# Weights in chunks of 768 columns, the second layer's by rows, half of them converted during attention

## Chip, cores and metric

One Trainium2 chip, one of its NeuronCores. The metric is the device time of one execution in microseconds. Engines are named TensorE (PE; PEld is its weight load), VectorE (DVE), ScalarE (ACT), GpSimd (POOL) and SyncE (SP, whose queue issues the transfers here).

## What is computed

Attention with a tanh cap over 2 batches, 12 heads, 448 positions and 64 channels; its output, 896 tokens by 768, goes through two feed-forward networks. All inputs are float32.

```python
scores = cap * np.tanh(scale * (q @ k.T) / cap)
attn = softmax(scores)                            # sum + 1e-9
x = (attn @ v) as [896, 768]

h = x @ w_in                                      # 768 -> 1024
solu = h * softmax(h)
ln = (solu - mean) / np.sqrt(var + 1e-6) * g_ln
x = ln @ w_out                                    # 1024 -> 768, the second layer

gate = sigmoid(x @ w_gate)                        # 768 -> 1536
out = (gate * (x @ w_val)) @ w_out2               # 1536 -> 768
```

## The kernel before

Every product of the networks is computed as three products of float32r operands (hi times hi, hi times lo, lo times hi), so weights and activations are split into a rounded upper part and the rest. The weights reach the kernel as 64-bit words. A chunk of 512 columns (`CH`, line 37) is loaded by SP into one of three raw buffers (`chunk_load`, line 308) and converted in six steps (`chunk_steps`, line 317): a mask of the upper word (line 349 on VectorE, or line 347 on ScalarE with `act=True`), a clamp (352), a shift (353), two merging steps on VectorE (354, 355), of which the second also rounds the upper part on ScalarE (`upper`, 336), and the subtraction of the rounded part on VectorE (`lower`, 339). For the second layer's weights `upper` first multiplies by the norm's weight `g_ln` on VectorE (334), since a chunk holds four blocks of 128 rows side by side for one block of 128 outputs. There are 12 chunks of w_in, 12 of w_mid (the second layer's weights), 36 of w_gv (gate and value) and 18 of w_fin.

`chunk_stream` (361) puts the steps of several chunks, interleaved, into a queue `todo`, and `fill(k)` issues the next k of them. A load goes out at the last step of the chunk three before it (`AHEAD`).

Attention (from line 520) runs in slots, two per pair of heads, each with half of the keys of that pair: scores on TensorE (`s_mm`), tanh and exp on ScalarE, the weighted sums on TensorE (`s_pv`); at each odd slot the sums are copied out (`s_out`) and turned into reciprocals through small transfers (`n_recip`), and GpSimd multiplies (`n_mult`). Slots 0 to 15 issue 5 conversion steps each (`FILL`), which are those of w_in. In slot 16 the stream of w_mid starts and five slots issue one step each. From slot 16 on the first layer of token tiles 0 and 1 runs beside attention (`beside`).

The loop over token tiles 2 to 6 (line 587) does the first layer's 36 products for a tile, then the maximum (`ln_max`), exp (`ln_exp`, line 420), the product h times exp (423), statistics, the norm (`ln_norm`, 441), and one tile later the transposes (`ln_trans`, 449) and the split into ln_hi and ln_lo (`ln_evac`). The buffer of exp and norm is a single one, so a tile's exp waits for the transposes of the tile before. Each round issues four conversion steps: after 18 of the products, after `ln_exp`, after `x_split` of the tile two ahead (on GpSimd, 392), and after `ln_norm`; tile 6 has its own order.

The second layer (`l2`, line 637) computes one block of 128 outputs for one of two token groups (384 and 512 columns), 24 products each. It needs the two chunks of its output block and calls `fill` until they are there, and 4 more steps after its products. Up to line 666 the order of the instructions on TensorE, ScalarE, VectorE and GpSimd is the order of the code; SP's order and all that follows (`load_slabs`, the gated layer, the last layer) is ordered by the compiler's planner.

Of the kernel before, what the change touches and what calls it, by code (L numbers as in the profile page):

```python
# [10 lines left out]
F32 = mybir.dt.float32  # L11
# [25 lines left out]
CH = 4 * P  # L37
# [6 lines left out]
AHEAD = 3  # L44
W2_BUFS = 9
# [8 lines left out]
FILL = 5  # L54
S_W2 = 16
FILL_T = 1
FILL_2 = 4
# [24 lines left out]
def fused_kernel(ctx: ExitStack, tc: tile.TileContext, qk, v, cap, w_in, w_mid, g_ln, w_gv, w_fin, outT):  # L82
# [5 lines left out]
    sh.wraw = ctx.enter_context(tc.tile_pool(name="wraw", bufs=3, side="right"))  # L88
    sh.cvt = ctx.enter_context(tc.tile_pool(name="cvt", bufs=3, side="right"))
# [53 lines left out]
def network(ctx: ExitStack, tc: tile.TileContext, sh, general, w_in, w_mid, w_gv, w_fin, outT):  # L143
# [10 lines left out]
    lns = ExitStack()  # L154
    lnt1 = lns.enter_context(tc.tile_pool(name="lnt1" + sfx, bufs=1, side="right"))
# [3 lines left out]
    lin = lns.enter_context(tc.tile_pool(name="lin" + sfx, bufs=1, side="right"))  # L159
    lin2 = lns.enter_context(tc.tile_pool(name="lin2" + sfx, bufs=2, side="right"))  # L160
    wi, x0 = ExitStack(), ExitStack()
    wip = wi.enter_context(tc.tile_pool(name="wi" + sfx, bufs=1, side="left"))
    x0p = x0.enter_context(tc.tile_pool(name="x0" + sfx, bufs=1, side="left"))
    wi_hi = wip.tile([P, K1, F1], F32R, name="wi_hi")
    wi_lo = wip.tile([P, K1, F1], F32R, name="wi_lo")
    x_sb = [x0p.tile([P, NP, S], F32, name="x0"), lin.tile([P, NP, S], F32, name="x1")]
# [150 lines left out]
    def chunk_steps(get, dst, scale=None, act=False):  # L317
# [43 lines left out]
    def chunk_stream(chunks):  # L361
# [16 lines left out]
        todo.extend(step for _, _, step in sorted(order, key=lambda x: x[:2]))  # L378
# [16 lines left out]
    def l1_mms(t):  # L395
# [3 lines left out]
        def mm(half, kk, m):  # L399
# [4 lines left out]
            c = slice(half * 512, half * 512 + 512)  # L404
            nc.tensor.matmul(hts[t][:, half], l[:, kk], r[:, kk, c], start=(kk == 0 and m == 0), stop=(kk == K1 - 1 and m == 2))  # L405
# [60 lines left out]
    def wi_dst(kk, half):  # L466
        c = slice(half * CH, half * CH + CH)
        return lambda: (wi_hi[:, kk, c], wi_lo[:, kk, c], None)
# [5 lines left out]
    chunk_stream([(w_in[:, kk, h * CH:(h + 1) * CH], wi_dst(kk, h), None) for h in range(2) for kk in range(K1)])  # L474
# [31 lines left out]
    def w2_dst(m, c):  # L506
        def dst():
            hl = w2p.tile([P, 2, 4, P], F32R, tag="w", name="w_hl")
            return hl[:, 0].rearrange("p a b -> p (a b)"), hl[:, 1].rearrange("p a b -> p (a b)"), lambda: w2[m].append(hl)
        return dst  # L510

    w2 = [[] for _ in range(K3)]
# [74 lines left out]
    for t in range(L1_BESIDE, 7):  # L587
        if t == 3:
            x0.close()
        if t == 2:  # L590
# [3 lines left out]
            w2p = lns.enter_context(tc.tile_pool(name="w2p" + sfx, bufs=W2_BUFS, side="right", reuse_waits="tile"))  # L594
# [12 lines left out]
        if t == 6:  # L607
# [4 lines left out]
            fill(3 * k)  # L612
# [12 lines left out]
        fill(k)  # L625
# [4 lines left out]


    def prod(out, w, kw, xh, xl, kx, first, last):
        wh, wl = w[kw // 4][:, 0, kw % 4], w[kw // 4][:, 1, kw % 4]
        for m, (l, r) in enumerate(((wh, xh), (wh, xl), (wl, xh))):
            nc.tensor.matmul(out, l, r[kx], start=(first and m == 0), stop=(last and m == 2))  # L635

    def l2(m, g):
        while len(w2[m]) < 2:
            fill(1)
# [28 lines left out]
    def load_slabs(src, pool):  # L668
# [3 lines left out]
        for c in range(src.shape[1] // 4):  # L672
            hl = pool.tile([P, 2, 4, P], F32R, tag="w", name="w_hl")
# [85 lines left out]
```

## Time and profile before

| | us |
|---|---|
| median of 3 runs | 514.84 |
| lowest and highest | 513.87, 514.85 |
| the profiled execution, its own time | 515.4 |
| its span, first to last instruction | 513.5 |
| PE busy | 495.0 (96%) |
| VectorE busy | 336.4 (66%) |
| ScalarE busy | 239.2 (47%) |

The profile is one execution. Busy times are of its span; what lies outside the span is 1.9 us. A matmul counts as busy from its start to its modelled end, and neighbours overlap, so the pace is read from the starts. "Idle before" names what the engine waited for. The granted clock is that of TensorE, 1.00 at its upper level of 2.4 GHz.

### The profile page before, as it was taken

The numbers are of one execution on the slowest core, as the hardware profiler recorded it, in microseconds if no ns is written. First come the engines' busy times: TensorE is split into PE (matmuls) and PEld (weight loads), VectorE is DVE, ScalarE is ACT, GpSimd is POOL, SyncE is SP. The second block draws the span as 40 slices with busy tenths as digits, with TensorE's granted clock in tenths as the row PEclk, the third lists the DMA queues.
The fourth block names the chain that finished last, engine by engine and source line by source line (L and its number), as shares of the span: only waits on it lengthen the run. The fifth ranks groups of instructions, "written<-read, shape, count | busy, mean of one in ns | idle before, by whom it ended". The sixth has DMA issues, their size and how long they took to land.

```text
span 513.5 us, 6510 instructions
## 1 busy us (share of the span) xinstructions
PE 495.0 (96%) x2480; PEld 386.8 (75%) x2480; DVE 336.4 (66%) x580; ACT 239.2 (47%) x326; POOL 57.1 (11%) x41
## 2 busy tenths in 40 slices
PE   8999999999998977999999999999999999999995
PEld 4333333553776767899899999999999999999995
DVE  1776854174788888569889888887877777551000
ACT  5999999575243432124454444434334433321000
POOL 0010101021212100000002111111111011000000
PEclk9999999999999997999999999999999999999999
DMA  7676665010101113115555444343333443500001
GB/s 253 185 214 178 207 184 157 18 38 19 61 0 41 42 43 122 58 66 165 168 160 171 141 140 123 124 123 92 106 93 122 124 123 101 158 37 37 19 36 41
DMA packets 19058, 55.04 MB, mean 107 GB/s; under 512 B 3212, under 2 KB 6156, under 8 KB 19020
## 3 DMA queue, kind: packets, MB, share of 16 engines
q1 hardware_dynamic: 19020, 54.56, 34.7%
q8 instruction: 21, 0.34, 0.3%
q14 instruction: 17, 0.14, 0.1%
HBM read 51.68 MB, written 2.79 MB: 106 GB/s over the span
## 4 chain that ended last, share of the span: by engine, by line
PE 76%; ACT 14%; DVE 7%; issue 2%; POOL 0%; ACTq 0%; POOLq 0%
PE big L635 34%; PE l4o L635 17%; PE l2o L635 11%; PE big L405 5%; ACT e L198 5%; ACT e L220 5%; PE big L192 3%; PE o L238 3%; DVE e L423 1%; ACT wi_hi L336 1%; DVE lnlo L456 1%; PE big L449 1%; PE sums L246 1%; ACT e L420 1%; PE warm L125 1%
## 5 line engine op out<-in xcount | busy, mean ns | idle before, releaser
L635 PE MATMUL big<-y_hi,w_hl 128*128 128x448 f32 x576 | 161.7, 362 | 0.0
L635 PEld LDWEIGHTS big<-y_hi,w_hl 128*128 128x128 f32 x576 | 107.9, 187 | 7.9
L635 PE MATMUL big<-y_lo,w_hl 128*128 128x448 f32 x288 | 104.6, 363 | 0.0
L336 ACT CAST w_hl<-cvt 128x512 fp32r<-128x512 f32 x66 | 40.8, 618 | 86.0 <-PE big L635 46.4
L635 PE MATMUL l4o<-p_hi,w_hl 128*128 128x448 f32 x288 | 80.7, 361 | 0.0
L355 DVE SCALAR_TENSOR_TENSOR cvt<-w_raw,cvt 128x512 uint32<-128x512 uint32 x78 | 72.8, 934 | 1.2
L635 PE MATMUL l2o<-lnhi,w_hl 128*128 128x384 f32 (+1 forms) x192 | 57.9, 379 | 6.3 <-DVE w_hl L339 6.3
L339 DVE TENSOR_TENSOR w_hl<-cvt,w_hl 128x512 fp32r<-128x512 f32 x66 | 45.3, 686 | 26.1 <-ACT w_hl L336 25.7
L347 ACT ACTIVATE cvt<-w_raw 128x512 f32<-128x512 f32 x54 | 36.2, 671 | 49.5 <-DVE w_hl L339 29.8
L635 PEld LDWEIGHTS l4o<-p_hi,w_hl 128*128 128x128 f32 x288 | 54.0, 187 | 3.9
L635 PEld LDWEIGHTS big<-y_lo,w_hl 128*128 128x128 f32 x288 | 54.1, 188 | 3.1
L354 DVE SCALAR_TENSOR_TENSOR cvt<-w_raw,cvt 128x512 uint32<-128x512 uint32 x78 | 53.6, 687 | 1.4
L708 POOL TENSOR_TENSOR p_lo<-sg,p_hi 128x896 fp32r<-128x896 f32 x12 | 30.5, 2538 | 210.7 <-ACT p_hi L707 210.7
L198 ACT ACTIVATE e<-big,cap_inv 112x896 f32<-112x896 f32 x48 | 46.6, 1038 | 14.8 <-PE big L192 14.8
L635 PE MATMUL l4o<-p_lo,w_hl 128*128 128x448 f32 x144 | 52.3, 363 | 0.0
L352 DVE TENSOR_SCALAR cvt<-cvt 128x512 f32<-128x512 f32 x78 | 33.7, 433 | 22.5 <-ACT cvt L347 22.3
L220 ACT ACTIVATE e<-e,cap_abs 112x896 f32<-112x896 f32 x48 | 48.1, 1073 | 0.0
L635 PEld LDWEIGHTS l2o<-lnhi,w_hl 128*128 128x128 f32 x192 | 37.2, 197 | 11.3 <-DVE w_hl L339 7.2
L238 PE MATMUL o<-e,v 112*64 112x448 f32 x192 | 43.4, 552 | 0.4 <-ACT to L254 0.3
L192 PE MATMUL big<-qk_raw 64*112 64x448 f32 x192 | 43.0, 559 | 0.3 <-ACT e L198 0.3
L353 DVE TENSOR_SCALAR cvt<-cvt 128x512 uint32<-128x512 uint32 x78 | 37.0, 476 | 1.6
L635 PE MATMUL l2o<-lnlo,w_hl 128*128 128x384 f32 (+1 forms) x96 | 36.0, 375 | 0.0
(81 smaller groups left out, 497.5 us busy)
## 6 DMA issues: line engine op xcount, KB each, us to landing
w_raw<-in_w_gv SPq DMA_DIRECT2D x36, 512.0 KB, 3.7
w_raw<-in_w_fin SPq DMA_DIRECT2D x18, 512.0 KB, 3.6
w_raw<-in_w_in SPq DMA_DIRECT2D x12, 512.0 KB, 4.2
w_raw<-in_w_mid SPq DMA_DIRECT2D x12, 512.0 KB, 4.9
qk_raw<-in_qk SPq DMA_DIRECT2D x12, 448.0 KB, 4.3
v<-in_v SPq DMA_DIRECT2D x12, 224.0 KB, 4.1
out_t<-ob SPq DMA_DIRECT2D x12, 224.0 KB, 2.3
qk_raw<-rd SPq DMA_DIRECT2D x22, 112.0 KB, 3.0
```

The lines of the kernel that those rows point to most:

```text
L192: nc.tensor.matmul(sc[j][:KC, c, :S], r[d, 1, kc * KC:(kc + 1) * KC], r[d, 0], start=True, stop=True)
L198: nc.scalar.activation(e, es[n, u][:KC, :, :S], AF.Tanh, scale=sh.cap_inv[:KC])
L220: nc.scalar.activation(es[n, u], es[n, u], AF.Exp, scale=sh.cap_abs[:KC])
L238: nc.tensor.matmul(o[d, :S], vs[i][:, kc, d], e[j][:, c], start=(kc == 0), stop=(kc == 3))
L336: nc.scalar.copy(st["hi"], w)
L339: v.tensor_tensor(st["lo"], st["w"], f32(st["hi"]), ALU.subtract)
L347: first = lambda t, lo, hi: nc.scalar.activation(f32(t), f32(hi), AF.Abs)
L352: word(lambda t, lo, hi: v.tensor_scalar(f32(t), f32(t), as_f32(W_MOST), as_f32(W_LEAST), ALU.min, ALU.max)),
L353: word(lambda t, lo, hi: v.tensor_scalar(t, t, 3, REST, ALU.logical_shift_left, ALU.bitwise_and)),
L354: word(lambda t, lo, hi: v.scalar_tensor_tensor(t, hi, TOP, t, ALU.bitwise_and, ALU.bitwise_or)),
L355: word(lambda t, lo, hi: (v.scalar_tensor_tensor(t, lo, 29, t, ALU.logical_shift_right, ALU.bitwise_or), upper())),
L635: nc.tensor.matmul(out, l, r[kx], start=(first and m == 0), stop=(last and m == 2))
```

## The change

Chunks become 768 columns wide, with two raw and two conversion buffers instead of three; there are 8 chunks of w_in, 8 of w_mid, 24 of w_gv and 12 of w_fin. A load goes out two chunks ahead, at the last step that reads the raw buffer. w_in is laid out so that a chunk is a run of 768 of its columns. A chunk of w_mid is one block of 128 rows with all 768 outputs, so that the norm's weight is one value per partition: it is applied as the scale of the rounding on ScalarE and inside the subtraction on VectorE, and the separate multiplication goes. Its mask step runs on ScalarE. The weights of the second layer stay in 8 buffers of their own, four of them (`w2a`) there from the start, four (`w2b`) from the end of attention. Slots 0 to 11 issue 4 steps each; the stream of w_mid starts in slot 12, and later slots issue 3 steps each, up to the rounding of the fifth chunk. The tile loop issues 5 steps per tile, and the fixed 4 steps in `l2` go. The x buffer of the second batch moves to the other side of the memory.

```diff
-CH = 4 * P
+CH = 6 * P
-AHEAD = 3
-W2_BUFS = 9
+AHEAD = 2
+
+W2_EARLY = 4
-FILL = 5
-S_W2 = 16
+FILL = 4
+S_W2 = 12
+FILL_W2 = 3
 FILL_T = 1
-FILL_2 = 4
...
-    sh.wraw = ctx.enter_context(tc.tile_pool(name="wraw", bufs=3, side="right"))
-    sh.cvt = ctx.enter_context(tc.tile_pool(name="cvt", bufs=3, side="right"))
+    sh.wraw = ctx.enter_context(tc.tile_pool(name="wraw", bufs=2, side="right"))
+    sh.cvt = ctx.enter_context(tc.tile_pool(name="cvt", bufs=2, side="right"))
...
         def upper():
-            w = f32(st["t"]) if wide else get()
-            if scale is not None:
-                wv = w.rearrange("p (a b) -> p a b", b=P)
-                v.tensor_tensor(wv, wv, scale[:, :, None].to_broadcast([P, CH // P, P]), ALU.mult)
-            st["w"], (st["hi"], st["lo"], st["done"]) = w, dst()
-            nc.scalar.copy(st["hi"], w)
+            st["w"] = f32(st["t"]) if wide else get()
+            st["hi"], st["lo"], st["done"] = dst()
+            if scale is None:
+                nc.scalar.copy(st["hi"], st["w"])
+            else:
+                nc.scalar.activation(st["hi"], st["w"], AF.Identity, scale=scale)
 
         def lower():
-            v.tensor_tensor(st["lo"], st["w"], f32(st["hi"]), ALU.subtract)
+            if scale is None:
+                v.tensor_tensor(st["lo"], st["w"], f32(st["hi"]), ALU.subtract)
+            else:
+                v.scalar_tensor_tensor(st["lo"], st["w"], scale, f32(st["hi"]), ALU.mult, ALU.subtract)
...
-            steps = chunk_steps(lambda c=c: raw[c], dst, scale)
-            last = steps[-1]
-            steps[-1] = lambda last=last, c=c: (last(), load(c + AHEAD))
+            steps = chunk_steps(lambda c=c: raw[c], dst, scale, act)
             n = len(steps)
-            order += [(n // 2 * c + k + 2 * (k == n - 1), c, step) for k, step in enumerate(steps)]
+            done = n - 2 if wide else n - 1
+            f = steps[done]
+            steps[done] = lambda f=f, c=c: (f(), load(c + AHEAD))
+            order += [(n // 2 * c + k + (k == n - 1), c, k == n - 2, step) for k, step in enumerate(steps)]
...
     def w2_stream():
-        chunk_stream([
-            (w_mid[m].rearrange("p a b -> p (a b)")[:, c * CH:(c + 1) * CH], w2_dst(m, c), sh.g_sb[:, c * 4:c * 4 + 4])
-            for m in range(K3) for c in range(2)
-        ])
+        return chunk_stream([(w_mid[kk], w2_dst(kk), sh.g_sb[:, kk:kk + 1]) for kk in range(K2)], act=True)
...
         elif s == S_W2:
             fill(len(todo))
-            w2_stream()
-        elif S_W2 < s < S_W2 + 6 and wide:
-            fill(s < S_W2 + 6)
+            w2_left = w2_stream()[W2_EARLY]
+        elif s > S_W2 and not general:
+            k = min(FILL_W2, w2_left)
+            w2_left -= k
+            fill(k)
...
             ln_norm(t, True)
-            fill(3 * k)
+            fill(4 * k)
             continue
...
         ln_norm(t, True)
-        fill(k)
+        fill(2 * k)
...
     def l2(m, g):
-        while len(w2[m]) < 2:
-            fill(1)
...
         for kk in range(K2):
-            prod(o[:, :n], w2[m], kk, ln_hi[g], ln_lo[g], (slice(None), kk), kk == 0, kk == K2 - 1)
+            while len(w2) <= kk:
+                fill(1)
+            w = [w2[kk][:, z, m * P:(m + 1) * P] for z in range(2)]
+            prods(o[:, :n], w, ln_hi[g][:, kk], ln_lo[g][:, kk], kk == 0, kk == K2 - 1)
         run(y_evac)
-        fill(FILL_2 if wide else 0)
...
-    w3p = ctx.enter_context(tc.tile_pool(name="w3p" + sfx, bufs=3, side="left", reuse_waits="tile"))
+    w3p = ctx.enter_context(tc.tile_pool(name="w3p" + sfx, bufs=2, side="left", reuse_waits="tile"))
...
-    w4p = ctx.enter_context(tc.tile_pool(name="w4p" + sfx, bufs=9, side="right", reuse_waits="tile"))
+    w4p = ctx.enter_context(tc.tile_pool(name="w4p" + sfx, bufs=6, side="right", reuse_waits="tile"))
```

## Rows read from the trace of the kernel before

**Rows 1.** Windows, last stages: PE, PEld, DVE, ACT, POOL busy, clock, DMA, GB/s.

```profile
251.40:508.50 257.10, 256.96 (x1284) 240.38 (x1283) 165.91 (x255) 89.44 (x134) 30.45 (x12) 1.00 0.35 106
```

**Rows 2.** Timeline, PE, 179 to 204 us: start, length, line, operation, tiles, [wait].

```profile
179.74 0.42 PE L635 MATMUL l2o<-lnhi,w_hl 128*128 128x384 f32 x1
...
181.24 0.52 PE L635 MATMUL l2o<-lnhi,w_hl 128*128 128x384 f32 x2
...
181.77 0.51 PE L635 MATMUL l2o<-lnhi,w_hl 128*128 128x384 f32 x2
...
196.68 1.01 PE L635 MATMUL l2o<-lnhi,w_hl 128*128 128x384 f32 x2 [2.95 <-DVE w_hl L339]
...
203.67 0.39 PE L635 MATMUL l2o<-lnlo,w_hl 128*128 128x512 f32 x1
```

**Rows 3.** Groups by shape: count, busy us, mean ns of one, idle before.

```profile
L347 ACT ACTIVATE cvt<-w_raw 128x512 f32<-128x512 f32 x54 | 36.2, 671 | 49.5 <-DVE w_hl L339 29.8 <-DMA w_raw<-in_w_gv 12.0 <-DVE cvt L355 4.3
...
L635 PE MATMUL l2o<-lnhi,w_hl 128*128 128x384 f32 x96 | 28.5, 369 | 6.3 <-DVE w_hl L339 6.3
...
L650 DVE TENSOR_TENSOR y_lo<-l2o,y_hi 128x512 fp32r<-128x512 f32 x6 | 4.1, 689 | 7.6 <-ACT y_hi L649 7.6
...
L650 DVE TENSOR_TENSOR y_lo<-l2o,y_hi 128x384 fp32r<-128x384 f32 x6 | 3.3, 553 | 1.3 <-ACT y_hi L649 1.3
```

**Rows 4.** Windows for PE: length, busy (instructions), clock, DMA share, GB/s.

```profile
196.68:203.30 6.62, 6.62 (x22) 0.53 0.36 110
```

**Rows 5.** The chain that ended last, 60 to 200 us: start, length, what.

```profile
62.49 0.51 ACT wi_hi L336
...
63.43 1.81 ACT e L198 x2
65.24 1.86 ACT e L220 x2
...
123.84 0.73 ACT xh L391
...
192.51 0.89 PE big L449 x8
```

**Rows 6.** Timeline, ACT, token tile loop and start of the second layer.

```profile
140.40 1.12 ACT L420 ACTIVATE e<-big,st 128x1024 f32<-128x1024 f32 x1 [1.59 <-DVE st L415]
...
180.46 1.12 ACT L420 ACTIVATE e<-big,st 128x1024 f32<-128x1024 f32 x1 [1.62 <-DVE st L415]
...
186.10 1.24 ACT L441 ACTIVATE e<-e,st 128x1024 f32<-128x1024 f32 x1 [3.52 <-DVE st L439]
```

**Rows 7.** Timeline, DVE, attention and token tile loop.

```profile
29.15 0.67 DVE L355 SCALAR_TENSOR_TENSOR cvt<-w_raw,cvt 128x512 uint32<-128x512 uint32 x1
...
84.83 0.96 DVE L392 TENSOR_TENSOR xl<-x,xh 128x768 fp32r<-128x768 f32 x1 [4.80 <-ACT xh L391]
...
145.80 1.67 DVE L353 TENSOR_SCALAR cvt<-cvt 128x512 uint32<-128x512 uint32 x1
```

**Rows 8.** Timeline, PE, first product that reads xl.

```profile
87.56 0.40 PE L405 MATMUL big<-wi_hi,xl 128*128 128x512 f32 x1
```

**Rows 9.** Transfers from 20 to 75 us: rate in 40 slices; count, KB, landing us.

```profile
GB/s 4 86 295 0 39 220 296 225 169 164 319 134 374 112 282 145 180 273 138 5 128 305 193 291 231 251 206 167 5 149 128 405 383 292 90 112 168 341 97 5
...
w_raw<-in_w_in SPq DMA_DIRECT2D x8, 512.0 KB, 4.2
```

**Rows 10.** The page's transfers: count, KB of one, us to landing.

```profile
w_raw<-in_w_fin SPq DMA_DIRECT2D x18, 512.0 KB, 3.6
...
out_t<-ob SPq DMA_DIRECT2D x12, 224.0 KB, 2.3
```

**Rows 11.** Timeline, SP, the queue that issues the transfers.

```profile
30.52 1.17 SPq L269 DMA_DIRECT2D qk_raw<-rd  x2
31.78 2.90 SPq L311 DMA_DIRECT2D w_raw<-in_w_in  x2
```

**Rows 12.** Timeline, POOL, a split of x.

```profile
145.34 1.84 POOL L392 TENSOR_TENSOR xl<-x,xh 128x768 fp32r<-128x768 f32 x1
```

More of the change, by code (lines that the diff above doesn't have):

```diff
@@ L162, in network @@
     wip = wi.enter_context(tc.tile_pool(name="wi" + sfx, bufs=1, side="left"))
+    x1p = wi.enter_context(tc.tile_pool(name="x1" + sfx, bufs=1, side="left"))
     x0p = x0.enter_context(tc.tile_pool(name="x0" + sfx, bufs=1, side="left"))
-    wi_hi = wip.tile([P, K1, F1], F32R, name="wi_hi")
-    wi_lo = wip.tile([P, K1, F1], F32R, name="wi_lo")
-    x_sb = [x0p.tile([P, NP, S], F32, name="x0"), lin.tile([P, NP, S], F32, name="x1")]
+    wi_hi = wip.tile([P, 2, K1, 512], F32R, name="wi_hi")
+    wi_lo = wip.tile([P, 2, K1, 512], F32R, name="wi_lo")
+    x_sb = [x0p.tile([P, NP, S], F32, name="x0"), x1p.tile([P, NP, S], F32, name="x1")]
     att = ExitStack()
@@ L359, in chunk_steps, with chunk_stream @@
         return steps + [lower]
-    def chunk_stream(chunks):
+    def chunk_stream(chunks, act=False):
         raw = {}
@@ L403, in mm @@
             l, r = ((xh, wi_hi), (xh, wi_lo), (xl, wi_hi))[m]
-            c = slice(half * 512, half * 512 + 512)
-            nc.tensor.matmul(hts[t][:, half], l[:, kk], r[:, kk, c], start=(kk == 0 and m == 0), stop=(kk == K1 - 1 and m == 2))
+            nc.tensor.matmul(hts[t][:, half], l[:, kk], r[:, half, kk], start=(kk == 0 and m == 0), stop=(kk == K1 - 1 and m == 2))
         for half in range(2):
@@ L464, in load_qk, with wi_dst @@
             raws[i] = sh.load(i, a3)
-    def wi_dst(kk, half):
-        c = slice(half * CH, half * CH + CH)
-        return lambda: (wi_hi[:, kk, c], wi_lo[:, kk, c], None)
+    def wi_dst(c):
+        hi, lo = (w.rearrange("p h k n -> p (h k n)")[:, c * CH:(c + 1) * CH] for w in (wi_hi, wi_lo))
+        return lambda: (hi, lo, None)
     v_load(0)
@@ L473, in network @@
         load_qk(i + 2)
-    chunk_stream([(w_in[:, kk, h * CH:(h + 1) * CH], wi_dst(kk, h), None) for h in range(2) for kk in range(K1)])
+    chunk_stream([(w_in[:, c * CH:(c + 1) * CH], wi_dst(c), None) for c in range(K1 * F1 // CH)])
     beside = {}
@@ L504, in network, with w2_dst @@
             at(s1, 2, x_split, t + 1)
-    def w2_dst(m, c):
+    def w2_dst(kk):
         def dst():
-            hl = w2p.tile([P, 2, 4, P], F32R, tag="w", name="w_hl")
-            return hl[:, 0].rearrange("p a b -> p (a b)"), hl[:, 1].rearrange("p a b -> p (a b)"), lambda: w2[m].append(hl)
+            pool = w2a if kk < W2_EARLY else w2b
+            hl = pool.tile([P, 2, DM], F32R, tag="w", name="w_hl")
+            return hl[:, 0], hl[:, 1], lambda: w2.append(hl)
         return dst
-    w2 = [[] for _ in range(K3)]
+    w2 = []
     def w2_stream():
-        chunk_stream([
-            (w_mid[m].rearrange("p a b -> p (a b)")[:, c * CH:(c + 1) * CH], w2_dst(m, c), sh.g_sb[:, c * 4:c * 4 + 4])
-            for m in range(K3) for c in range(2)
-        ])
+        return chunk_stream([(w_mid[kk], w2_dst(kk), sh.g_sb[:, kk:kk + 1]) for kk in range(K2)], act=True)
     NS = 2 * NPAIR
@@ L629, in network, with prods @@
     y_lo = ytp.tile([P, K3, NT], F32R, name="y_lo")
[L632 to L635, printed above, removed]
+    def prods(out, w, xh, xl, first, last):
+        for m, (l, r) in enumerate(((w[0], xh), (w[0], xl), (w[1], xh))):
+            nc.tensor.matmul(out, l, r, start=(first and m == 0), stop=(last and m == 2))
     def l2(m, g):
-        while len(w2[m]) < 2:
-            fill(1)
         t0, t1 = GROUPS[g]
@@ L671, in load_slabs @@
         flat = src.rearrange("p a b -> p (a b)")
-        for c in range(src.shape[1] // 4):
-            hl = pool.tile([P, 2, 4, P], F32R, tag="w", name="w_hl")
+        for c in range(src.shape[1] * P // CH):
+            hl = pool.tile([P, 2, CH // P, P], F32R, tag="w", name="w_hl")
             parts = hl[:, 0].rearrange("p a b -> p (a b)"), hl[:, 1].rearrange("p a b -> p (a b)"), None
@@ L700, in network @@
                 for kk in range(K3):
-                    prod(o[:, hf, :HT], w, z * K3 + kk, y_hi, y_lo, (slice(None), kk, slice(hf * HT, hf * HT + HT)), kk == 0, kk == K3 - 1)
+                    c = slice(hf * HT, hf * HT + HT)
+                    prods(o[:, hf, :HT], part(w, z * K3 + kk), y_hi[:, kk, c], y_lo[:, kk, c], kk == 0, kk == K3 - 1)
             gv.append(o)
@@ L719, in network @@
             for kk in range(K4):
-                prod(o[:, :HT], w, kk, p_hi, p_lo, (slice(None), kk, c), kk == 0, kk == K4 - 1)
+                prods(o[:, :HT], part(w, kk), p_hi[:, kk, c], p_lo[:, kk, c], kk == 0, kk == K4 - 1)
             ob = tl.tile([P, HT], F32, tag="sg", name="ob")
```

18 lines of the change are left out of this document (11 added, 7 removed).

## The prediction, made before the change was run

> **What bounds the kernel now.** I read the busy time by stage first. From 251.40 on (the gated layer and the last one) TensorE is busy 256.96 of 257.10 us [rows 1]: no edit to the conversions can shorten that stretch, it can only start sooner. So the question is when the unbroken matmul stream begins, and next I read TensorE's timeline where the second layer starts [rows 2]. Its first block runs from 179.74, three matmuls in 0.53 us. Then TensorE waits three times, 6.3 us together, for the VectorE subtraction (L339) that finishes a chunk of the second layer's weights [rows 3]; the last wait ends at 196.68 [rows 2]. The granted clock from there to 203.30 is 0.53, mostly the lower of its two levels (1.2 GHz), after those gaps [rows 4]. Before 179.74 two chains rule: ScalarE's tanh and exp during attention [rows 5], then, tile by tile, exp, product, statistics, norm and transposes, each tile's exp behind the transposes of the one before.
>
> **What the second layer gains.** Now the first output block needs only two chunks, and the others are converted beside the matmuls, too slowly. After the change each of the 8 chunks is one 128-row slice over all 768 outputs, so the first block needs all 8; I therefore counted the steps. A chunk has 6. w_in's 48 go into slots 0 to 11, 4 each. The 48 of w_mid start in slot 13, 3 per slot, and stop ahead of the fifth chunk's rounding: 29 steps, which slots 13 to 22 take. That leaves 19. The tile loop takes 5 per tile for t = 2 to 5, so the last (the eighth chunk's subtraction) is queued on VectorE before tile 6's maximum, and none is left for the second layer. The three waits cannot occur any more. From 179.74 to about 203.45, just ahead of the row at 203.67, lie 72 products of 384 columns [rows 2] and 8 transposes, 0.89 us [rows 5]: 24 x 0.53 + 0.89 = 13.6 us of work in 23.7 us. That is **-10.0 us**, waits, restarts and slow clock together. What is late next there: the transposes of tile 6. TensorE reaches them two blocks (8.5 us) after 179.74, at 188.2; the norm of tile 6 ends at 186.10 + 1.24 = 187.3 [rows 6], and no conversion is left on its path, so 0.9 us of slack remains.
>
> **What attention pays.** (1) ScalarE. A slot holds two tanh and two exp, 1.81 + 1.86 us, and each 512-column rounding adds 0.51 on the chain; the 768-column rounding of x costs 0.73 there [rows 5]. So w_in's rounding goes from 12 x 0.51 = 6.1 to 8 x 0.73 = 5.8 us, but is finished three slots sooner. Into slots 13 to 16 come three ScalarE masks (the Abs that replaces a VectorE step for w_mid) and two scaled roundings. Abs of 512 columns is 0.67 us in its row [rows 3], some 0.57 without overlap; 256 columns more at the roundings' slope (0.73 - 0.51) make it 0.79. The rounding with a per-partition scale has no row; tanh over 896 columns takes such a scale and 1.81 / 2 = 0.90, which the same slope brings to 0.80 at 768 (the ends: 0.73 and 0.90). That is 3 x 0.79 + 2 x 0.80 = 4.0, so ScalarE ends slot 16 by 5.8 + 4.0 - 6.1 = 3.7 us later. Not all of it arrives: VectorE's split of x for tile 0 ends at 84.83 + 0.96 = 85.8, and its first product is at 87.56, so 1.8 us of it fall into slack [rows 7, 8]. From there slots with first-layer matmuls take over 6 us of TensorE against some 3.7 + 1.6 of ScalarE, so the later masks and roundings hide. **+1.8 us** (1.5 to 3.7). (2) In slot 22 one Abs stands ahead of the rounding of x for tile 2, which is on the chain at 123.84 [rows 5]. Behind it wait VectorE's split and tile 1's maximum: **+0.5 us** (0.2 to 0.8).
>
> (3) The loads, where I see the largest risk. Three raw buffers of 512 columns become two of 768. VectorE's order is then: last word step of chunk c, ..., first step of c+2, last word step of c+1. The load of c+2 starts only when the last word step of c has freed its buffer. So each chunk needs one landing plus two VectorE steps, a mask (some 0.5 us) and a two-operand step, 0.69 at 512 columns and with 553 to 689 ns per 128 columns some 0.87 without overlap at 768 [rows 3]. ScalarE's pace for a chunk is 1.5 slots with their share of copies and roundings, about 6.55 us. A 512 KB load lands after 4.2 us in this stage [rows 9]. For 256 KB more: 0.65 us at the fastest rate of a slice (405 GB/s) [rows 9], 1.2 us at the slope between the 224 KB and 512 KB transfers (2.3 and 3.6 us) [rows 10]. So 4.85 to 5.4; I take 5.0, nearer to the row of the same stage. With 0.1 to issue that gives 6.45 us, just inside the pace. But SP's queue is in order: the load at 31.78 leaves behind the two broadcasts of 30.52, though its buffer's last reader ended at 29.15 + 0.67 [rows 7, 11]. After the change I find one load (fifth chunk, slot 4) behind such a pair, 1.4 us late, and a first wait of 0.4 us in slot 2, as the first chunk is larger. VectorE waits, the rounding waits for VectorE, and ScalarE's next tanh is queued behind the rounding. **+2.0 us** (0.3 to 7).
>
> The Trainium skill ("DMA: Bandwidth & Descriptors", section "Anatomy of one DMA") models a transfer as a fixed part of some 2 us and bytes at 436 GB/s, for another issuing path; by it 256 KB more would cost an estimated 0.6 us, the lower end above. The rows agree that much of a load is fixed time; no row shows 768 KB.
>
> **What the tile loop pays.** It runs from 140.40 (tile 2's exp) to 180.46 (tile 6's), four rounds of 10.0 us [rows 6]. VectorE had 16 conversion steps of 512 columns there and three multiplications by the norm's weight; it gets 17 steps of 768, two Abs more being ScalarE's. A two-operand step costs some 0.27 more, a single one 0.13. One step per tile stands ahead of the norm while GpSimd splits x: there the step at 145.80 takes 1.67 us and ends 0.29 after GpSimd's (145.34 + 1.84) [rows 7, 12]. I sum the chain by round, with masks and shifts at 0.47 to 0.59 and the rest at 0.87. Tile 2 to 3: the two steps behind the norm and the maximum now outlast norm and transposes, +0.6. Tile 3 to 4: -0.3, as a single step replaces a word step, a multiplication and a rounding ahead of the norm. Tiles 4 to 5 and 5 to 6: +0.55 and +0.65, where a word step and a rounding of 768 columns stand there. **+1.5 us** (0 to 4, the upper end if 15 steps add 0.27 in full). By the Trainium skill ("SBUF — State Buffer", section "Who interferes with whom") the two engines share a port under an exclusive lock, and the later one blocks in full. By that only the part after GpSimd's end grows, 0.1 to 0.3 us a tile, as summed; were it a share of bandwidth, the 1.67 would grow by half, 0.8 a tile and some 2.5 us over three tiles. That the step ends 0.29 after GpSimd agrees with the lock.
>
> **At nothing.** The multiplication by the norm's weight (12 VectorE instructions) goes; the weight is in the rounding and the subtraction. With it gone and 52 chunks for 78, VectorE is freer in the last two layers, but TensorE covers all of it [rows 1]; if that cover failed, a slab's two chunks (some 9 us of VectorE) would still fit its 72 products of 0.2 us. The first slab of the gated layer is converted on a VectorE that has nothing else left. Later slabs reuse the space of the second layer's weights, free only in its last block; the first of them is wanted 14 us later.
>
> **The sum.** -10.0 + 1.8 + 0.5 + 2.0 + 1.5 = -4.2 us on the profiled 515.4: 511.2. The median of the runs before, 514.84, is 0.56 lower, so 510.6; the rivals below are given against the median too.
>
> **The rivals.** (A) *Loads don't pace attention* (landing at 4.85 us, none stuck behind a broadcast): term 3 is 0.3, the time 508.9. For it: VectorE waits for no such load now beyond the first; against: the third buffer that hid them goes. (B) *Loads pace attention*, the slower side: with 5.4 us to land and a mean 0.85 us stuck in SP's queue a chunk takes 7.7 us, 1.17 over the pace; over six chunks and the first wait that is 7.4 for term 3, the time 516.0. It decides from landing plus queue of about 6.1 us, where term 3 eats the other terms' 6.2. For it: every link of that loop is in order; against: 4.2 us now. (C) *The tile loop takes the gain*: wider steps add in full (+4.0) and the attention terms reach 6: about 515, no change. For it: VectorE is on that chain in most of its pieces; against: half of the steps lie beside norm, transposes and exp. That the change doesn't do what it says would need conversions left over at the second layer's start; the step count excludes it.
>
> **How the numbers follow.** Forecast 0.60 (508.2 to 513.2), A and better 0.16, B 0.13, C 0.11. A measurement of this kernel can tell about 0.2%, 1 us, from no change, so the bounds are 513.8 and 515.9. Faster: 0.60 + 0.16 = 0.76. Same: most of C and the edge of B, 0.12. Slower: the rest of B and C's tail, 0.12. The range that leaves out 2 in 10 runs from 507.3 (A with the tile loop at nothing) to 515.2.
>
> **What would show it.** Right: no wait for L339 after the second layer's first matmul, a clock of 1.00 there, that matmul near 185.5, and some 59 us from it to the last one of the layer. Term 3: VectorE's first step waiting for the load of w_in, and ScalarE's rounding for VectorE; B if more than 5 us of it. Tile loop: rounds of 10.3, 10.8, 11.0 and 9.5 us. Wrong: a clock that falls in the tile loop, where TensorE's gaps grow, so that the second layer starts at the lower level, or a late first slab of the gated layer.

## The result, and the profile after it

The changed kernel takes 521.73 us in the median of 4 runs (520.79 to 523.24), the kernel before 514.85 beside it: the ratio is 1.014, 95% interval 1.0111 to 1.0168. The forecast was 510.6. The profiled execution of the changed kernel took 522.07 us with a span of 520.3; before it was 515.4 with 513.5.

The table compares the two traces by stretch. Attention issues its tanh in 24 pairs, one per slot; "pair n" counts them from 0, and pair n is issued in slot n-1. "Exp t" is the exp of the first layer's token tile t. All are start times on ScalarE, and the last column ends with the last matmul on TensorE. (The expectations quoted below name these stretches by slot or by pair; the figure beside each says which is meant.)

| stretch | before | after | difference |
|---|---|---|---|
| start to pair 2 | 15.33 | 16.08 | +0.75 |
| pair 2 to pair 13 (w_in is converted) | 47.91 | 50.61 | +2.70 |
| pair 13 to pair 18 (new: w_mid's first steps) | 21.46 | 25.16 | +3.70 |
| pair 18 to exp 2 | 55.70 | 56.11 | +0.41 |
| exp 2 to exp 6 (tile loop) | 40.06 | 44.74 | +4.68 |
| exp 6 to the last matmul | 327.90 | 322.42 | -5.48 |
| last matmul ends at | 508.36 | 515.12 | +6.76 |

So the second layer did start to gain, but 5.5 us and not 10.0, and every stretch ahead of it is longer. I do not count the first stretch to the change: its whole difference is there at the first tanh already (7.18 and 7.94), ahead of every conversion, and in the runs below, whose code is the same up to there but for the order of some loads, it lay between 15.01 and 16.34.

Where the second layer's gain went is seen on the two engines that convert. Lines are those of the changed kernel: L352 is the mask (Abs) on ScalarE, L357 to L360 are VectorE's four word steps, L336 and L338 the plain and the scaled rounding, L342 and L344 the plain and the scaled subtraction, L429 a tile's exp, L432 to L443 product and statistics, L450 the norm, L458 the transposes. First ScalarE's timeline (start, length, line, operation, tiles, and in brackets the wait ahead of it with what ended it):

```profile
188.53 1.24 ACT L450 ACTIVATE e<-e,st 128x1024 f32<-128x1024 f32 x1
189.68 0.82 ACT L336 CAST w_hl<-cvt 128x768 fp32r<-128x768 f32 x1
191.89 0.91 ACT L352 ACTIVATE cvt<-w_raw 128x768 f32<-128x768 f32 x1 [1.39 <-DMA w_raw<-in_w_gv]
192.70 1.09 ACT L429 ACTIVATE e<-big,st 128x1024 f32<-128x1024 f32 x1
...
199.75 0.83 ACT L336 CAST w_hl<-cvt 128x768 fp32r<-128x768 f32 x1 [4.10 <-DVE cvt L360]
201.95 1.24 ACT L450 ACTIVATE e<-e,st 128x1024 f32<-128x1024 f32 x1 [1.36 <-DVE st L448]
```

Between tile 5's norm (188.53) and tile 6's exp (192.70) stands an L352 that waits for a load of the gated layer's weights, in_w_gv. In the kernel before, ScalarE went from tile 5's norm at 177.59 straight to the exp at 180.46, and tile 6's norm followed 5.64 us behind that [rows 6]; now it is 9.25 us behind. The row of tile 5's norm before:

```profile
177.59 1.25 ACT L441 ACTIVATE e<-e,st 128x1024 f32<-128x1024 f32 x1 [3.86 <-DVE st L439]
```

VectorE's timeline, in which the same two chunks are interleaved with tile 6's statistics:

```profile
191.34 0.95 DVE L342 TENSOR_TENSOR w_hl<-cvt,w_hl 128x768 fp32r<-128x768 f32 x1
192.83 0.56 DVE L357 TENSOR_SCALAR cvt<-cvt 128x768 f32<-128x768 f32 x1 [0.54 <-ACT cvt L352]
...
195.12 0.55 DVE L358 TENSOR_SCALAR cvt<-cvt 128x768 uint32<-128x768 uint32 x1
195.58 0.68 DVE L439 BATCH_NORM_STATS2 st<-e 128x6 f32<-128x512 f32 x1
...
197.36 0.95 DVE L359 SCALAR_TENSOR_TENSOR cvt<-w_raw,cvt 128x768 uint32<-128x768 uint32 x1
...
198.77 0.95 DVE L360 SCALAR_TENSOR_TENSOR cvt<-w_raw,cvt 128x768 uint32<-128x768 uint32 x1
199.63 0.15 DVE L443 TENSOR_TENSOR st<-st 128x1 f32<-128x1 f32 x1
...
200.84 0.95 DVE L359 SCALAR_TENSOR_TENSOR cvt<-w_raw,cvt 128x768 uint32<-128x768 uint32 x1
```

The chain that ended last runs through that load (start, length, what):

```profile
187.58 4.22 DMA w_raw<-in_w_gv
191.84 0.04 issue
191.89 0.06 ACT cvt L352
```

And TensorE, which finishes two blocks of the second layer with no wait for a weight and then needs tile 6's transposes:

```profile
203.24 1.09 PE L458 MATMUL big<-ident,e 128*128 128x128 f32 x8 [3.88 <-ACT e L450]
```

The windows of TensorE (length, busy with count, granted clock, DMA share, GB/s) around it:

```profile
190.67:199.30 8.63, 8.63 (x51) 1.00 0.34 116
199.30:203.24 3.94, 0.06 (x1) 1.00 0.60 186
203.24:207.70 4.46, 4.46 (x20) 0.64 0.61 189
207.70:258.50 50.80, 50.80 (x245) 1.00 0.05 16
```

The three waits of [rows 3] and the slow stretch of [rows 4] are gone, as forecast. In their place stand one idle stretch of 3.9 us and 4.46 us at a clock of 0.64, part of it at the lower level.

### The profile page after: what moved, and what is told of

The parts are those of the page before. It is cut to its first block, busy times and chain, and to the rows that moved or that the text cites. A ratio compares the mean times of both kernels' runs of the same rounds, so it can differ in the third digit from the quotient of the medians.

```text
span 520.3 us, 6249 instructions
## 1 busy us (share of the span) xinstructions
PE 497.3 (96%) x2480; PEld 387.4 (74%) x2480; DVE 311.5 (60%) x422; ACT 237.2 (46%) x290; POOL 53.6 (10%) x41
## 4 chain that ended last, share of the span: by engine, by line
PE 69%; DVE 12%; ACT 12%; DMA 3%; issue 3%; POOL 0%; ACTq 0%; DVEq 0%; POOLq 0%; SPq 0%
PE big L641 33%; PE l4o L641 17%; PE l2o L641 10%; ACT e L200 4%; ACT e L222 3%; PE big L414 3%; PE big L194 2%; DMA w_raw<-in_w_in 2%; DVE cvt L360 2%; PE o L240 2%; DVE e L432 2%; DVE st L424 1%; ACT e L429 1%; DVE cvt L359 1%; DVE lnlo L465 1%
## 5 line engine op out<-in xcount | busy, mean ns | idle before, releaser
L357 DVE TENSOR_SCALAR cvt<-cvt 128x768 f32<-128x768 f32 x52 | 42.2, 812 | 34.5 <-ACT cvt L352 34.3
L360 DVE SCALAR_TENSOR_TENSOR cvt<-w_raw,cvt 128x768 uint32<-128x768 uint32 x52 | 53.8, 1035 | 1.1
L352 ACT ACTIVATE cvt<-w_raw 128x768 f32<-128x768 f32 x44 | 39.7, 902 | 32.4 <-DMA w_raw<-in_w_gv 16.6
L336 ACT CAST w_hl<-cvt 128x768 fp32r<-128x768 f32 x36 | 30.0, 833 | 49.3 <-PE big L641 29.5
L342 DVE TENSOR_TENSOR w_hl<-cvt,w_hl 128x768 fp32r<-128x768 f32 x36 | 34.3, 953 | 30.4 <-ACT w_hl L336 30.3
L359 DVE SCALAR_TENSOR_TENSOR cvt<-w_raw,cvt 128x768 uint32<-128x768 uint32 x52 | 49.5, 952 | 1.0
L240 PE MATMUL o<-e,v 112*64 112x448 f32 x192 | 44.8, 553 | 3.1 <-ACT to L256 1.9
L720 POOL TENSOR_TENSOR p_lo<-sg,p_hi 128x896 fp32r<-128x896 f32 x12 | 26.2, 2181 | 206.5 <-ACT p_hi L719 206.5
L194 PE MATMUL big<-qk_raw 64*112 64x448 f32 x192 | 44.7, 563 | 0.6 <-ACT e L200 0.3
L194 PEld LDWEIGHTS big<-qk_raw 64*112 64x112 f32 x192 | 16.3, 174 | 27.8 <-issue 19.9
L240 PEld LDWEIGHTS o<-e,v 112*64 112x64 f32 x192 | 13.8, 136 | 30.6 <-issue 14.3
```

Of the source, the lines that this page charges most:

```text
L194: nc.tensor.matmul(sc[j][:KC, c, :S], r[d, 1, kc * KC:(kc + 1) * KC], r[d, 0], start=True, stop=True)
L240: nc.tensor.matmul(o[d, :S], vs[i][:, kc, d], e[j][:, c], start=(kc == 0), stop=(kc == 3))
L336: nc.scalar.copy(st["hi"], st["w"])
L352: first = lambda t, lo, hi: nc.scalar.activation(f32(t), f32(hi), AF.Abs)
L357: word(lambda t, lo, hi: v.tensor_scalar(f32(t), f32(t), as_f32(W_MOST), as_f32(W_LEAST), ALU.min, ALU.max)),
L359: word(lambda t, lo, hi: v.scalar_tensor_tensor(t, hi, TOP, t, ALU.bitwise_and, ALU.bitwise_or)),
```

## The experiments

My theory after this comparison: outside the order that is written by hand, a planner places the gated layer's conversions. The second layer's conversions now end earlier, their buffers come free earlier, and the planner moves the first gated chunks up, into the in-order queues of VectorE and ScalarE, ahead of tile 6's exp, statistics and norm. The rival is that the wide steps of the change, or tile 6's own chain, are late whatever stands there. Four runs stand beside the changed kernel with one edit each (the second has two), and six more build on the first. Code is shown in parts; "..." marks what is left out.

**e1, the first gated slab put in order by hand.**

```
+    fill(len(todo))
     l2(2, 0)
+    w3p = ctx.enter_context(tc.tile_pool(name="w3p" + sfx, bufs=2, side="left", reuse_waits="tile"))
+    w3 = [slab_steps(w_gv[0], w3p)]
...
         run(y_evac)
+        if g or m > 2:
+            fill(2)
...
```

`slab_steps` issues the slab's two loads and appends the 12 steps of its chunks to the queue `todo`.

> The first slab of the gated layer's weights (two chunks, 12 steps) is put into the hand-written order, two steps after each block of the second layer, from the third block on; nothing else differs from the changed kernel. Theory 1 (the loss in the tile loop and at the second layer's start is the planner's: it sets these steps, and the wait for their load, ahead of tile 6's exp, statistics and norm on the two in-order engines): the exp of tile 6 comes about 9.5 us after that of tile 5 instead of 12.23, TensorE no longer waits 3.88 us for tile 6's norm, and the time falls by 8 to 9 us, from 521.7 to about 513. Rival (the wider steps of the change itself, or tile 6's own chain, are late whatever stands between): the round stays near 12 us and the time between 519 and 522.

Measured: 515.47 us, ratio 1.001 (1.000 to 1.002). That is 6.26 us under the changed kernel, for the place of 12 steps: the two loads leave SP as before the edit (at 177.59 and 187.60 us, for 176.89 and 187.58), and only the steps move, the slab's roundings from 189.68 and 199.75 to 218.13 and 234.10. From exp 6 to the last matmul it takes 317.90 us, 10.00 less than before: the forecast for the second layer (that it fits to the digit is luck; e5 to e10 take 317.26 to 318.32). TensorE no longer waits from the second layer's first product on:

```profile
191.19:253.20 62.01, 62.01 (x314) 1.00 0.17 51
```

Tile 6's exp and norm are 5.63 us apart again:

```profile
191.94 1.12 ACT L429 ACTIVATE e<-big,st 128x1024 f32<-128x1024 f32 x1 [2.31 <-DVE st L424]
...
197.57 1.24 ACT L450 ACTIVATE e<-e,st 128x1024 f32<-128x1024 f32 x1 [3.52 <-DVE st L448]
```

The theory holds and the rival falls, but I had priced it some 2 us too high. The round from exp 5 to exp 6 is 10.76 us, not 9.5. The window behind tile 4's transposes, for which TensorE had waited 2.72 us, shows one reason:

```profile
179.68:185.00 5.32, 5.32 (x21) 0.68 0.27 109
185.00:190.40 5.40, 5.40 (x26) 1.00 0.33 83
```

At full clock 5.32 us at 0.68 would be 3.6, an estimate; in e7 below the same place stays at 1.00, and the round takes 9.68. The fall of the clock was one of the signs I had named for a wrong forecast.

**e2, a third raw buffer while w_in is converted** (and, to make room, three early chunks of w_mid instead of four).

```
-W2_EARLY = 4
+W2_EARLY = 3
...
+    wx = att.enter_context(tc.tile_pool(name="wx" + sfx, bufs=1, side="right"))
...
-                raw[c] = chunk_load(chunks[c][0])
+                raw[c] = chunk_load(chunks[c][0], third if third and c % 3 == 2 else wraw)
...
```

> During attention the first layer's weight chunks get a third raw buffer and are loaded three ahead; to make room, three instead of four chunks of the second layer's weights are converted during attention. The stretch to read is from the second tanh to that of slot 12, before the second layer's weights begin: 47.91 us in the kernel before, 50.61 in the changed one. Theory 1 (two raw buffers pace the chunks: a buffer comes free too late for a load of 5 to 6 us to land in time): VectorE's waits for these loads vanish after the first, and the stretch returns to 48 to 48.7 us. Rival (the engines' own steps pace it): it stays at 50 to 50.7. For the whole run the first gives about 519 (the one chunk fewer in attention saves at most another 1.7 us of ScalarE there and costs as much later), the second 520 to 522.5.

Measured: 521.91 us (ratio 1.0147, 1.0128 to 1.0166). In the changed kernel VectorE's first step of a chunk (L354) waits for w_in's load three times after the first:

```profile
42.99 0.57 DVE L354 TENSOR_SCALAR cvt<-w_raw 128x768 uint32<-128x768 uint32 x1 [1.00 <-DMA w_raw<-in_w_in]
51.25 0.56 DVE L354 TENSOR_SCALAR cvt<-w_raw 128x768 uint32<-128x768 uint32 x1 [1.00 <-DMA w_raw<-in_w_in]
59.56 0.57 DVE L354 TENSOR_SCALAR cvt<-w_raw 128x768 uint32<-128x768 uint32 x1 [2.86 <-DMA w_raw<-in_w_in]
```

and SP's queue shows the last two of these loads leaving right behind a pair of broadcasts:

```profile
43.89 1.16 SPq L271 DMA_DIRECT2D qk_raw<-rd  x2
45.14 0.53 SPq L313 DMA_DIRECT2D w_raw<-in_w_in  x1
...
52.41 1.16 SPq L271 DMA_DIRECT2D qk_raw<-rd  x2
53.66 0.53 SPq L313 DMA_DIRECT2D w_raw<-in_w_in  x1
```

With the third buffer only the first wait is left, and the stretch is 48.83 us, just above the 48 to 48.7 of the theory: the loads cost 1.78 here. The attention theory holds, but the whole time that I gave with it, 519, does not: the 3.0 us that exp 2 comes earlier (144.94 for 147.96) are lost at the other end. With 23 instead of 29 steps taken in attention, the tile loop finishes the rest only behind tile 6's norm, and the second layer waits for its weights again, now in line L345 and L339 (this kernel's numbers for the scaled subtraction and rounding):

```profile
193.25 0.45 PE L644 MATMUL l2o<-lnhi,w_hl 128*128 128x384 f32 x1 [3.55 <-DVE w_hl L345]
196.07 0.69 PE L644 MATMUL l2o<-lnhi,w_hl 128*128 128x384 f32 x1 [2.38 <-ACT w_hl L339]
```

From exp 6 to the end it takes 327.45 us, all but the 327.90 of before. So the gain of the second layer hangs on a margin of at most 6 steps. The planner's place for the slab moved too: here its first rounding comes at 200.18, behind tile 6's norm (192.30), and the round from exp 5 to exp 6 is 9.49 us. In e3 and e4 below, which take all 29 steps in attention, the first rounding is ahead of that norm again, and the round is 12.28 and 12.18.

**e3, no step of w_mid in slots 13 to 16, five a slot afterwards.**

```
-            k = min(FILL_W2, w2_left)
+            k = min(0 if s < S_L1 + 1 else 5, w2_left)
```

> No conversion step of the second layer's weights in slots 13 to 16; five a slot instead of three from slot 17 on, where TensorE carries the first layer's products beside attention. Theory 1 (in slots 13 to 16 ScalarE paces, so each mask and rounding set into them is paid for in full, and from slot 17 TensorE paces, so that they are hidden): the stretch from the tanh of slot 12 to that of slot 17, 25.16 us in the changed kernel and 21.46 before, falls to about 21.5 to 22, and the total by 2 to 3.5 us, to 518 to 520. Rival (the steps only move: VectorE and ScalarE have no more room from slot 17 on, above all in slots 20 and 21 where the first layer's normalisation stands): the gain is given back by the exp of tile 2, and the total stays at 520.5 to 523.

Measured: 527.66 us (1.0261, 1.0236 to 1.0286). Pair 13 to pair 18 takes 21.61 us, close to the 21.46 of before: without steps there 3.55 us are gone. But pair 18 to exp 2 goes from 56.11 to 64.39. The rival holds, and with a price that I had not seen: the time is 4.7 us above its range. In slot 20 VectorE starts tile 0's product (L432), which empties the accumulators, at 115.87, with four of the five steps ahead of it; its exp began at 110.93 and took 1.12. Behind that product the scores, and behind those the tanh, wait:

```profile
115.87 1.22 DVE L432 TENSOR_TENSOR e<-big,e 128x1024 f32<-128x1024 f32 x1
```

```profile
119.03 1.01 ACT L200 ACTIVATE e<-big,cap_inv 112x896 f32<-112x896 f32 x1 [3.43 <-PE big L194]
```

Pair 21 to pair 22 takes 10.81 us there, 6.84 in the changed kernel with two steps ahead of the product, 6.29 before with one step of 512 columns. That is 4 of the 8.3 us; another 2.3 come right behind it, where the granted clock from 116.89 to 123.71 is 0.50 and pair 22 to pair 23 takes 10.18 us for 7.90.

**e4, the same steps behind each slot's other work.**

```
         elif s > S_W2 and not general:
-            k = min(FILL_W2, w2_left)
-            w2_left -= k
-            fill(k)
+            pass
...
         phase(s, 2)
         phase(s, 3)
+        if s > S_W2 and not general:
+            k = min(FILL_W2, w2_left)
+            w2_left -= k
+            fill(k)
```

> The same steps in the same slots, but each slot's come behind the slot's evictions and the first layer's norm steps instead of ahead of them. Theory 1 (in slot 20 two conversion steps stand ahead of the product that empties the first tile's accumulators, and so hold a buffer that the scores of slot 22 wait for): that product starts at once behind its exp, TensorE's scores of slot 22 do not wait for it, the exp of tile 2 comes 1 to 1.5 us earlier, and the total falls by about 1.2 us, to 520 to 520.8. Rival (what the steps delay is something else that is equally on the path): no change, 521.2 to 522.5, or slower where the steps now hold up the scores' exponentials.

Measured: 524.63 us (1.0179, 1.0156 to 1.0201), slower than the changed kernel. The theory falls: tile 0's product comes 2.84 us behind the start of its exp (116.84 for 114.00), no earlier than in the changed kernel (2.71), since the steps of slot 19 now stand between. And the steps behind the product end late, and a rounding on ScalarE waits for them with the next tanh queued behind it:

```profile
123.60 0.94 ACT L338 ACTIVATE w_hl<-cvt,g_sb 128x768 fp32r<-128x768 f32 x1 [5.75 <-DVE cvt L360]
124.44 1.89 ACT L200 ACTIVATE e<-big,cap_inv 112x896 f32<-112x896 f32 x2
```

Pair 21 to pair 22 is 12.24 us, and the same happens in an earlier slot (a wait of 2.80 us, pair 13 to pair 18 at 27.72). So the steps have two deadlines: they must not stand ahead of the product (e3, e6), nor come so late that a rounding with a tanh behind it waits for them (e4).

**e5, e1 with a third raw buffer that costs no room.** It lies in the space of the second batch's attention output, and four chunks stay early.

```
+            if spare:
+                r = x_sb[1].rearrange("p a b -> p (a b)")[:, :2 * CH].bitcast(U32).rearrange("p (n two) -> p n two", two=2)
...
```

> The gated layer's first slab in the hand-written order, as in the first run, and during the first layer's conversions a third raw buffer that lies in the space of the second batch's attention output, not written before slot 17; four chunks of the second layer's weights in attention, as in the changed kernel. Theory (two raw buffers cost 1.8 us of the stretch from the tanh of slot 1 to that of slot 12, and a gain there reaches the end): that stretch is 48.6 to 49 us instead of 50.61, and the time 1.8 us under that of the first run, 513.3 to 514. Rival (what is gained there is lost again behind it, as it was with the steps of slots 13 to 16 when they were moved): 515 to 516.

Measured: 513.62 us, ratio 0.9981 (0.9967 to 0.9994); pair 2 to pair 13 takes 48.85 us. The 1.8 us are there, and reach the end.

**e6, e5 without steps in slot 20.** The queue moves by a slot, so its last two steps come in slot 23.

```
-            k = min(FILL_W2, w2_left)
+            k = min(0 if s == S_W2 + 8 else FILL_W2, w2_left)
```

> The kernel of the run before with one more edit: no conversion step of the second layer's weights in slot 20, so that the product which empties the first tile's accumulators follows its exp at once; its three steps come in slot 21. Theory (the two steps ahead of that product hold the buffer for which the scores of slot 22 wait, 1.2 to 1.4 us from the tanh of slot 21 to the exp of tile 2, as three chunks instead of four in attention gave back 36.66 less 35.23): that stretch is 35.2 to 35.6 us instead of 36.7, and the time 512 to 513. Rival (the three steps cost the same in slot 21, where the statistics of the second tile and its exp stand): 36.5 us and 513.3 to 514.5.

Measured: 512.60 us (0.9968, 0.9953 to 0.9982). Pair 21 to pair 22 is 6.29 us as before the change, 0.54 less than in e5; pair 21 to exp 2 is 36.18, where I had expected 35.2 to 35.6. So two steps ahead of the product cost 0.54 us and not 1.2. The 35.23 of e2, from which I took that price, has no step in slots 21 and 22 at all. That the medians lie 1.0 apart is not this edit alone: e5's trace has a fall of the clock in the tile loop (43.25 us for 41.92).

**e7, e5 with the masks of the four early chunks on VectorE.**

```
-            steps = chunk_steps(lambda c=c: raw[c], dst, scale, act)
+            steps = chunk_steps(lambda c=c: raw[c], dst, scale, act and c >= W2_EARLY)
```

> The kernel with the third buffer and the hand-written order, and the first step of each of the four chunks that are converted during attention (the mask of the upper word) on VectorE instead of ScalarE. Theory (in slots 13 to 16 ScalarE paces and VectorE has room: four masks of 0.92 us lie in slots 13 to 20): the stretch from the tanh of slot 13 to that of slot 18, 25.16 us in the changed kernel and 21.46 before, falls by 1.5 to 3 us, and the time is 511 to 512.5. Rival (each rounding on ScalarE stands ahead of the next tanh and waits for the chain of VectorE's steps, so a longer chain there costs as much as the mask saves): 25 us again, 513.3 to 514.5, or slower.

Measured: 510.55 us (0.9920, 0.9903 to 0.9937). Pair 13 to pair 18 falls from 24.74 to 22.51. In these slots ScalarE sets the pace: three masks lie there, and 2.23 us come back.

**e8, the edits of e1, e5, e6 and e7 together.**

> All four edits together: the hand-written order for the gated layer's first slab, the third raw buffer, no step in slot 20, the masks of the early chunks on VectorE. If each of the three theories holds and the gains add up (1.8, 1.3 and 1.5 to 3 us under the first run's 515.5): 509.4 to 511, faster than both kernels. If the gains in attention are taken back by the slot that follows: 513 to 515.

Measured: 511.10 us (0.9921, 0.9895 to 0.9947), no better than e7. Exp 2 comes at 143.22 (144.70 in e7), but the tile loop takes 43.20 us (41.91), with a granted clock of 0.90 and 0.94 in its last two rounds and 1.00 in e7's. Of the 1.48 us ahead of exp 2 only 0.65 lie behind pair 18, where the edit is; 0.79 are the stretch of w_in, in which the same code scatters as much. In the profiled executions the clock took most of that back; the medians can't tell e7 and e8 apart.

**e9 and e10, in the tile loop the step that stood ahead of the norm behind it;** e9 on e8, e10 on e7.

```
-        fill(k)
         ln_norm(t, True)
-        fill(2 * k)
+        fill(3 * k)
```

> The kernel with all four edits, and in the tile loop the conversion step that stood between a tile's statistics and its norm comes behind the norm. Theory (that step is on the path: on VectorE it stands ahead of the small product that the norm waits for, and beside GpSimd's work it took 1.80, 1.80, 2.27 and 0.95 us, while TensorE waited 0.94, 1.06 and 2.72 us for the norm): these waits vanish, the four rounds from the exp of tile 2 to that of tile 6 take 39 to 40.5 us together instead of 43.20 (40.06 in the kernel before), and the time falls by 2.5 to 4 us, to 507 to 508.6. Rival (the step only moves, and holds up the maximum of the next tile or a weight of the second layer): 42 to 43 us, and 510.5 to 511.5.

> The same move of the step behind the norm, on the kernel that keeps the three steps in slot 20 (the hand-written order, the third buffer, the masks of the early chunks on VectorE), which took 510.55. Theory: rounds of 39 to 40.5 us together instead of 41.91, and 508 to 509.5. Rival: 510.5.

Measured: e9 509.55 us (0.9899, 0.9881 to 0.9917) and e10 510.05 (0.9905, 0.9888 to 0.9923). The rounds take 42.01 and 42.03 us: the theory's 39 to 40.5 falls. The longest of TensorE's waits for a norm does shrink; first e7, then e9:

```profile
175.73 1.09 PE L463 MATMUL big<-ident,e 128*128 128x128 f32 x8 [2.73 <-ACT e L455]
```

```profile
172.26 1.09 PE L463 MATMUL big<-ident,e 128*128 128x128 f32 x8 [1.54 <-ACT e L455]
183.18 1.09 PE L463 MATMUL big<-ident,e 128*128 128x128 f32 x8 [1.63 <-ACT e L455]
```

But the steps now hold up the next tile's maximum (L429 in e9), and its exp waits:

```profile
173.98 1.02 DVE L347 SCALAR_TENSOR_TENSOR w_hl<-cvt,g_sb,w_hl 128x768 fp32r<-128x768 f32 x1
174.92 1.22 DVE L429 TENSOR_REDUCE st<-big 128x1 f32<-128x1024 f32 x1
```

```profile
176.25 1.12 ACT L434 ACTIVATE e<-big,st 128x1024 f32<-128x1024 f32 x1 [2.30 <-DVE st L429]
```

The step moves along a chain that is full. Both kernels are 1% faster than the one before, and the clock stayed at 1.00 in every round of e9. Its median is the lowest of all, though its interval and those of e7, e8 and e10 overlap.

## Why the prediction was wrong, step by step

The miss is 11.1 us (521.73 for 510.6). The runs split it.

**The step that failed: "at nothing".** I wrote that the first slab of the gated layer is converted on a VectorE that has nothing else left. I looked at the last two layers, where TensorE covers all [rows 1], and not at where the planner would put the slab once its buffers came free earlier. I did name "a late first slab" as a sign, but what came was an early one. Moving its 12 steps gave back 6.26 us (e1), over half of the miss, though their loads stayed where they were.

**The second layer, -10.0: right as a mechanism and in size.** The waits for L339 [rows 2, 3] are gone, and once the planner's steps are out of the way the stretch behind exp 6 is 10.00 us shorter. (The "some 59 us" that I named from the layer's first matmul to its last don't follow from that sum: 251.40 - 179.74 - 10.0 is 61.7, and e1 shows 61.69.) The step count held too: e2 shows that with 6 steps fewer in attention the waits come back. The 0.9 us of slack for tile 6 was a true figure for an order that the built kernel did not have: in e1 the norm ends at 198.81 and the transposes start at 199.70.

**ScalarE in attention, +1.8 (1.5 to 3.7): mis-sized.** The instructions were priced well. The page's groups by shape (count, busy us, mean ns, idle before) give 939 ns for the scaled rounding and 902 for the mask, overlap included:

```profile
L352 ACT ACTIVATE cvt<-w_raw 128x768 f32<-128x768 f32 x44 | 39.7, 902 | 32.4 <-DMA w_raw<-in_w_gv 16.6 <-DVE w_hl L342 15.8
...
L338 ACT ACTIVATE w_hl<-cvt,g_sb 128x768 fp32r<-128x768 f32 x8 | 7.5, 939 | 10.1 <-DVE cvt L360 10.1
```

On the chain they are shorter: in slot 16 a mask starts at 89.51, the rounding behind it at 90.31 and the next instruction at 91.13, so 0.80 and 0.82 where I had 0.79 and 0.80. The rest was not. With the 0.94 that the stretch of w_in costs beside its loads (2.70 less the 1.76 that e5's buffer returned) 0.94 + 3.70 = 4.64 us come by pair 18 where I had summed 3.7; ScalarE's waits between pairs 13 and 18, which had no term, are 1.04 us (0.72 of it for scores, at 71.22), 0.21 before. And of the 3.70 us in pairs 13 to 18 only 1.07 disappear by pair 19 (5.98 us for 7.05), not 1.8. So the term is 4.64 - 1.07 = 3.57 us, near the upper end that I had given and not taken.

**The loads, +2.0 (0.3 to 7): right, 1.76 by e5.** (The same code took 50.61 to 51.16 us for this stretch in four executions, and with the third buffer 48.80 to 49.61 in seven, so 1.0 to 2.4.) The mechanism is the one described: a buffer that comes free while SP issues two broadcasts, then a landing. From the issue at 45.14 to VectorE's start at 51.25 are 6.1 us, from 53.66 to 59.56 5.9, from one at 38.03 to 42.99 5.0. My 5.0 was the lowest of these three, and two loads instead of one stood behind broadcasts; but no more than three chunks waited. By the Trainium skill ("DMA: Bandwidth & Descriptors", section "Anatomy of one DMA") the added 256 KB would cost 0.6 us over the 4.2 of [rows 9], an estimate of 4.8. The 5.0 is near it, and the eight landings that the traces of e2 and e5 to e10 record for such loads in this stage, 4.25 to 5.59 us, lie around it; the 5.9 and 6.1 do not agree.

**Slot 22, +0.5: too small.** Pair 19 to exp 2 cost 1.48. I had costed the mask ahead of x's rounding, but not the two VectorE steps ahead of tile 0's product, which holds a buffer that the scores need. e6 shows 0.54 for that, and e3 4.5 us (10.81 for 6.29) when there are four. The other 0.94 no run took apart.

**The tile loop, +1.5 (0 to 4): three rounds right, the last not.** I gave 10.3, 10.8, 11.0 and 9.5 us; the changed kernel shows 10.37, 10.84, 11.30 and 12.23. Without the planner's steps the last is 9.68 (e7) to 10.76 (e1); the sum is then 1.85 us over before in e7 and 3.22 in e1, of which the last round's fall of the clock is about 1.1 (10.76 for 9.68). The shared port went as forecast. GpSimd's split of x and VectorE's step beside it, in the changed kernel:

```profile
152.91 1.84 POOL L402 TENSOR_TENSOR xl<-x,xh 128x768 fp32r<-128x768 f32 x1
```

```profile
153.36 1.80 DVE L358 TENSOR_SCALAR cvt<-cvt 128x768 uint32<-128x768 uint32 x1
```

The step ends 0.41 us after the split, where 512 columns ended 0.29 after it [rows 7, 12]: only the part behind GpSimd's end grew, by 0.12. That agrees with the exclusive lock of the Trainium skill ("SBUF — State Buffer", section "Who interferes with whom"), and not with a share of bandwidth.

**The sum, and the rivals.** The terms as measured in the changed kernel, 3.57 + 1.76 + 1.48 + 4.68 - 5.48, with the 0.75 of the start, give the +6.76 of the table. None of my rivals was this one. B (loads pace attention) came nearest with 516.0, by luck: its reason was worth 1.76 us and not 7.4. With the slab out of the way the time is that of e1, 515.47: within the measurement of no change, and just above my range. What is left of the miss there is several small costs, all but the loads on one side, each taken at the middle of its bounds or below.

What stays open: why the planner chose that place. That the buffers came free earlier is argued from the traces, and e2, where w_mid's steps end later and the slab stays behind tile 6's norm, points the same way; no run changed that alone.

## What to carry to other kernels

Work outside a hand-written order is not free because its engine looks idle there: when an edit frees buffers earlier, look up where a planner would now put the next loads and their consumers, and what stands behind them on an in-order engine. A step set into a full slot has a deadline on both sides: it must not stand ahead of whatever frees an accumulator, nor end so late that a rounding on another engine waits for it with the next critical instruction queued behind. When a sum is made of one large gain and several costs whose bounds reach further up than down, as here, take the costs nearer their upper ends.

## What the runs showed of the hardware

- The granted clock does not follow from the length of a gap alone. After TensorE's wait of 2.72 us in e1 it was 0.68 for 5.32 us. After one of 2.73 us at the same place in e7, the window that begins with the same transposes shows:

```profile
175.73:186.50 10.77, 10.35 (x53) 1.00 0.34 117
```

  Nine of the traces have that wait (2.70 to 2.73 us); the clock falls behind it in four (e1, e4, e5, e8). It looks as if one kernel goes both ways too: of e1's ten executions four (the profiled one, with the fall, among them) have a mean granted clock of 0.994 and take 515.80 to 516.79 us, six have 0.996 to 0.999 and take 513.84 to 515.62.

- The second layer without waits kept the clock up: from 191.19 to 253.20 it was 1.00 in e1, where the stretch of [rows 4] in the kernel before, behind three waits, was at 0.53.
- A VectorE step of 768 columns takes 0.56 us alone and 1.80 beside GpSimd's split of x, and a two-operand step 0.95 and 2.27 (the longest, in e1). They end 0.41 and 0.81 us behind GpSimd's instruction, somewhat less than their length alone: the step waits out the rest of the other engine's instruction.
